# An attention kernel with head mixing and a dense block: a batch's second block scored a step sooner in its middle unit, heads 8 to 11 first, keys a step sooner

## Chip, cores and metric

One core of a Trainium2 chip. The metric is the device time of one execution in microseconds (us); lower is better. Engines are TensorE (PE, matmuls), VectorE (DVE), ScalarE (ACT), GpSimd (POOL) and SyncE (SP, which here only issues transfers).

## What is computed

For 4 batches, 12 heads, 448 positions and 64 dimensions per head, attention scores are mixed over the heads before the softmax and the weights once more after it; the result goes through a dense block of 768 to 2048 to 768 with an ELU between.

```python
scores = scale * np.matmul(q, k.transpose(0, 1, 3, 2))
scores = np.einsum('bhij,hg->bgij', scores, w_pre)
attn = exp(scores - max); attn = attn / (sum(attn) + 1e-09)
attn = np.einsum('bhij,hg->bgij', attn, w_post)
x = np.matmul(attn, v)              # (batch, head, position, 64)
h = x.reshape(1792, 768) @ w_in     # positions by heads and dimensions
out = elu(h) @ w_out
```

## The kernel before

The dense block (class `Moe`) runs after the attention and isn't touched by the change; the rest of this section is on `attention`.

**Blocks and steps.** The 448 query positions of a batch are cut into four blocks of 100, 120, 120 and 108 positions (`BLK`, in tiles of 10 rows). A block is worked off in steps of two tiles; the last step of a batch's fourth block has one tile. A batch is thus 5 + 6 + 6 + 6 = 23 steps (`ROUND`), the four batches 92 steps. Step numbers in this document are those of the round, 0 to 22, where nothing else is said. Batches, blocks and heads are counted from 0; "block 2" of a batch is its third.

**What a block goes through.** First its raw scores: for each of the six pairs of heads `qk` (line 220) multiplies the block's queries by the batch's keys. Both are split into a high and a low part, so three matmuls make one product. Two pairs are a unit: unit 0 has heads 0 to 3, unit 1 heads 4 to 7, unit 2 heads 8 to 11. `keep_qk` (line 230) copies the four results of a unit from PSUM into `st` tiles, two on DVE, then two on ACT. In the next step `send` (lines 242 and 245) moves them by transfers from SP into one of the two tiles `raw`, where the head becomes part of the partition; blocks alternate between the two. Head 11 goes in two halves (line 245), so unit 2 takes five transfers and the others four. Then, step by step, `scores` (line 256) mixes the heads of two tiles out of `raw`, the maximum is taken on DVE (`nm`, line 261), the exponential on ACT (`p`, line 263), `norm` makes the scaled weights `wz` on POOL (line 276), and `post` (line 287) applies the second mixing. `keep_post` (line 294) copies it to `at`. Last, `av` (line 308, results `xo`) multiplies by the values `v`, again in three units per block, and `keep_av` writes the block out.

**The order of the work.** One loop over the step number `j` issues everything. In iteration `j` PE gets the scores of step `j + 2`, then the `av` units of `avs[j]`, then the `qk` units of `qks[j]`, then the post-mix of step `j`; the transfers of the units of iteration `j - 1` are issued by SP behind the scores. So the first scores of a block are issued two iterations ahead of its first step, and need all three units of the block to have landed in `raw`. Two tables set the iterations: `RAW_AT` (line 377) has, for each block of a batch, the iterations of its three `qk` units relative to the batch's first step, `OUT_AT` (line 378) those of its three `av` units. Results of scores, `qk` and `av` take six PSUM banks in turn (`bank`): a step's scores two, an `av` unit one, a `qk` unit four.

**Keys and queries.** For each batch after the first, `load_k` (line 179) loads the keys of a pair of heads on POOL's queue, into four buffers, five iterations ahead of the unit that needs it; `split_k` makes `kh` on DVE (line 185) and `kl` on POOL (line 186) two and one iterations ahead. Queries go likewise through `load_q` (line 191) and `split_q` (line 198). The `v` tiles of the next batch are loaded on POOL's queue in iterations 23 to 28 (0 to 5 of the next round), and from iteration 8 on a decoder of the dense block's weights loads 512 KB (`w`) every eighth iteration or so.

The line in which a block's units are given their iterations:

```python
for u in range(2 if n == 1 else 0, 3):
    qks.setdefault(at[u], []).append((n, u))
```

Of the kernel before, what the change touches and what calls it, by code (L numbers as in the profile page):

```python
# [27 lines left out]
NP = H // 2  # L28
# [14 lines left out]
def f32(ap):  # L43
    return ap.bitcast(F32)
# [67 lines left out]
@with_exitstack  # L112
def body(ctx, tc, qd, kd, vd, wpre, wpost, w1d, w2d, outT):
    xd = [[tc.dram_tile([128, NC, nt * R], F32, name=f"xd{b}_{i}") for i, (_, nt) in enumerate(BLK)]
          for b in range(B)]
    s1 = [tc.dram_tile([128, PW], F32, name=f"s1_{i}") for i in range(w1d.shape[0])]
    s2 = [tc.dram_tile([128, PW], F32, name=f"s2_{i}") for i in range(w2d.shape[0])]
    todo = [(d[i], s[i]) for d, s in ((w1d, s1), (w2d, s2)) for i in range(d.shape[0])]
    dec = Weights(tc.nc, ctx.enter_context(tc.tile_pool(name="dec", bufs=2, side="right")), todo, tc.nc.gpsimd)
    with tc.manual_schedule():  # L120
        moe = Moe(ctx, tc, xd, s1, s2, dec, outT)
        attention(tc, qd, kd, vd, wpre, wpost, xd, dec, moe)
        moe.run()
# [3 lines left out]
def attention(ctx, tc, qd, kd, vd, wpre, wpost, xd, dec, moe):  # L127
    nc = tc.nc
# [48 lines left out]
    def load_k(b, hp, eng):  # L177
        k2[b, hp] = ld.tile([128, S], F32, tag="k2", name="k2", bufs=4)
        eng.dma_start(out=k2[b, hp], in_=kd[b, hp])

    def split_k(b, hp, high, low):
        src = k2.pop((b, hp))
        kh = kp.tile([128, S], F32R, tag="kh", name="kh")
        kl = kp.tile([128, S], F32R, tag="kl", name="kl")
        high(kh, src)
        low.tensor_sub(kl, src, f32(kh))
        ks[b, hp] = kh, kl

    def load_q(n, eng):
        q2[n] = ld.tile([128, NP, 120], F32, tag="q2", name="q2")  # L190
        eng.dma_start(out=q2[n], in_=qd[blocks[n]])

    def split_q(n, high, low):
        src = q2.pop(n)
        qh = qp.tile([128, NP, 120], F32R, tag="qh", name="qh")
        ql = qp.tile([128, NP, 120], F32R, tag="ql", name="ql")
        high(qh, src)
        low.tensor_sub(ql, src, f32(qh))
        qs[n] = qh, ql
# [168 lines left out]
    work, qks, avs = {}, {}, {}  # L368
    spare = mixes = six

    def plan(j, f):
        work.setdefault(max(j, -LOOK), []).append(f)
# [1 line left out]


    ROUND = sum(length)  // B
    RAW_AT = [(-10, -8, -6), (-4, -2, -1), (1, 3, 5), (7, 9, 11)]
    OUT_AT = [(6, 8, 10), (12, 14, 16), (18, 20, 22), (23, 25, 27)]
    for n in range(1, NBL):
        b, i = blocks[n]  # L380
        at = [b * ROUND + j for j in (RAW_AT[i] if n > 2 else (None, (0, 0, 0), (2, 4, 6))[n])]
        for u in range(2 if n == 1 else 0, 3):
            qks.setdefault(at[u], []).append((n, u))
        if n > 1:
            plan(max(at[0] - 5, 1 - LOOK), lambda n=n: load_q(n, nc.gpsimd))
        if n > 1:
            plan(at[0] - 2, lambda n=n: split_q(n, nc.vector.tensor_copy, nc.gpsimd))
        if i == (0 if b else 2):
            for hp in range(NP):
                if b:  # L390
                    plan(at[hp // 2] - 5, lambda b=b, hp=hp: load_k(b, hp, nc.gpsimd))
                plan(at[hp // 2] - 2 + hp % 2, lambda b=b, hp=hp: split_k(
                    b, hp, nc.vector.tensor_copy, nc.gpsimd))
    for n in range(NBL):
        b, i = blocks[n]
        for u, j in enumerate(OUT_AT[i]):
            j += b * ROUND
# [725 lines left out]
```

## Time and profile before

| what | value |
|---|---|
| median of 3 runs | 813.8 us (808.64 to 817.66) |
| the profiled execution | 816.36 us |
| its span, first to last instruction | 814.6 us |
| mean granted TensorE clock | 0.983 |
| PE busy | 779.7 us, 96% |
| DVE, ACT, POOL busy | 582.2, 510.1, 407.9 us (71, 63, 50%) |

Attention takes about the first 360 us of the span, the dense block the rest. A matmul of the code on these four-byte operands stands in the trace as two records, so the four score matmuls of a step are counted x8, a post-mix x56, an `av` unit x32. In a timeline the columns are start, duration (of the merged group), engine, line, operation, result and operands, shapes and count; in brackets the engine's idle time ahead of it and what ended it. "issue" means that the profile shows nothing that the engine waited for. `SPq` and `POOLq` are the queues of engines that issue transfers.

### The profile page before, as it was taken

How to read it: one execution, taken by the hardware profiler on the slowest of the kernel's cores; microseconds unless marked ns; L12 is line 12 of the kernel's file. 1: busy time of each engine (PE TensorE's matmuls, PEld its weight loads, DVE VectorE, ACT ScalarE, POOL GpSimd, SP SyncE). 2: the span in 40 equal slices, each digit the busy share in tenths (PEclk: the TensorE clock that was granted, in tenths of full speed). 3: DMA queues.
4: the chain of work that ended last, by engine and by line, in shares of the span. 5: the costliest groups of instructions: out<-in, count | busy, mean ns of one | idle time of the engine just before them, and what ended most of it. 6: DMA issues, size and time to landing. Idle time of an engine off the chain costs nothing.

```text
span 814.6 us, 25153 instructions
## 1 busy us (share of the span) xinstructions
PE 779.7 (96%) x10014; PEld 633.0 (78%) x10014; DVE 582.2 (71%) x1082; ACT 510.1 (63%) x1092; POOL 407.9 (50%) x529
## 2 busy tenths in 40 slices
PE   7788899899999999999999999999999999999998
PEld 3356577566666676678999999999999889899997
DVE  5676577597768777666988888776457777688962
ACT  3567678577777778786778783323157566665440
POOL 6565445374456543345777773266148777600000
PEclk9799899899999999999999999999999999999999
DMA  6568568665777676756988769987536867553331
GB/s 197 182 205 254 165 197 241 209 210 189 222 248 232 191 217 224 213 170 232 311 307 277 249 232 356 313 293 275 184 124 202 260 200 231 185 161 119 115 122 58
DMA packets 92845, 174.60 MB, mean 214 GB/s; under 512 B 21888, under 2 KB 59556, under 8 KB 92728
## 3 DMA queue, kind: packets, MB, share of 16 engines
q1 hardware_dynamic: 75288, 113.46, 43.4%
q0 software_dynamic: 16896, 58.61, 22.7%
q8 instruction: 79, 1.29, 0.7%
q10 hardware_dynamic: 544, 0.92, 0.3%
q14 instruction: 38, 0.31, 0.1%
HBM read 94.04 MB, written 39.35 MB: 164 GB/s over the span
## 4 chain that ended last, share of the span: by engine, by line
PE 82%; DMA 9%; DVE 3%; issue 2%; POOL 2%; ACT 2%; SPq 1%; POOLq 0%; ACTq 0%; DVEq 0%
PE h L595 14%; PE y L690 14%; PE y L1044 13%; PE h L982 10%; PE mixed L287 8%; PE s L256 8%; PE xo L308 8%; PE qk L220 6%; DMA raw<-st 3%; DMA sum<-mix 1%; ACT p L263 1%; DMA raw<-room 1%; DMA mix<-s 1%; DMA xl<-xd 1%; DMA wa<-in 1%
## 5 line engine op out<-in xcount | busy, mean ns | idle before, releaser
L263 ACT ACTIVATE p<-s,nm 128x448 f32<-128x448 f32 x180 | 113.0, 634 | 58.7 <-DVE nm L261 58.3
L261 DVE TENSOR_REDUCE nm<-s 128x1 f32<-128x448 f32 x180 | 103.8, 617 | 59.4 <-PE s L256 59.0
L276 POOL TENSOR_SCALAR wz<-wb,rz 128x60 f32<-128x60 f32 x180 | 80.4, 459 | 106.8 <-DVE rz L272 63.5
L294 ACT COPY at<-mixed 128x480 f32<-128x480 f32 (+1 forms) x184 | 93.4, 567 | 32.1 <-PE mixed L287 30.2
L256 PE MATMUL s<-raw,wa 64*64 64x448 f32 x720 | 95.8, 571 | 18.1 <-DMA raw<-st 9.1
L287 PEld LDWEIGHTS mixed<-wz,p 64*64 64x64 f32 x5040 | 86.3, 137 | 32.7 <-issue 24.7
L287 PE MATMUL mixed<-wz,p 64*64 64x60 f32 x5040 | 99.8, 225 | 5.1 <-issue 3.4
L308 PEld LDWEIGHTS xo<-at,v 128*64 128x64 f32 x1536 | 76.1, 135 | 33.0 <-ACT st L230 21.8
L1044 PE MATMUL y<-part,hi 128*128 128x448 f32 x336 | 96.4, 367 | 0.0
L308 PE MATMUL xo<-at,v 128*64 128x120 f32 (+2 forms) x1536 | 87.1, 263 | 0.5 <-issue 0.5
L511 ACT CAST hi<-lo 128x1024 fp32r<-128x1024 f32 (+1 forms) x49 | 48.1, 982 | 40.5 <-PE y L1044 34.5
L982 PE MATMUL h<-op,hi 128*128 128x448 f32 x264 | 72.2, 367 | 0.0
L595 PE MATMUL h<-xh,hi 128*128 128x448 f32 x192 | 70.7, 368 | 0.0
L595 PE MATMUL h<-xl,hi 128*128 128x448 f32 x192 | 70.1, 365 | 0.0
L595 PE MATMUL h<-xh,lo 128*128 128x448 f32 x192 | 70.1, 365 | 0.0
L690 PE MATMUL y<-gl,hi 128*128 128x448 f32 x192 | 69.8, 363 | 0.0
L690 PE MATMUL y<-gh,hi 128*128 128x448 f32 x192 | 69.8, 363 | 0.0
L690 PE MATMUL y<-gh,lo 128*128 128x448 f32 x192 | 69.7, 363 | 0.0
L982 PE MATMUL h<-op,lo 128*128 128x448 f32 x240 | 67.5, 368 | 1.4 <-POOL lo L839 1.4
L1044 PEld LDWEIGHTS y<-part,hi 128*128 128x128 f32 x336 | 63.0, 188 | 6.3
L512 DVE TENSOR_TENSOR lo<-lo,hi 128x1024 fp32r<-128x1024 f32 x30 | 37.5, 1250 | 40.6 <-ACT hi L511 38.4
L1044 PE MATMUL y<-part,lo 128*128 128x448 f32 x168 | 61.8, 368 | 0.0
(122 smaller groups left out, 1659.0 us busy)
## 6 DMA issues: line engine op xcount, KB each, us to landing
raw<-st SPq DMA_DIRECT2D x129, 210.0 KB
w<-in POOLq DMA_DIRECT2D x48, 512.0 KB, 5.8
lo<-s SPq DMA_DIRECT2D x58, 256.0 KB
s<-c POOLq DMA_DIRECT2D x48, 256.0 KB, 5.6
v<-in POOLq DMA_DIRECT2D x24, 256.0 KB, 6.3
lo<-half SPq DMA_DIRECT2D x16, 384.0 KB
lo<-sum SPq DMA_DIRECT2D x12, 512.0 KB
raw<-st SPq DMA_DIRECT2D x33, 175.0 KB
```

The costliest lines, as they stand in the source:

```text
L220: nc.tensor.matmul(got[hh][:m, :S], q[part, hp, :m], k[part], start=i == 0, stop=i == 2)
L256: nc.tensor.matmul(ps[a][w * 64:(w + 1) * 64, :S], wa[half], raws[n % 2][half, ts[0] + w, :], start=True, stop=True)
L261: nc.vector.tensor_reduce(nm, ps[i][:, :S], op=ALU.max, axis=AX.X, negate=True)
L263: nc.scalar.activation(p, ps[i][:, :S], AF.Exp, bias=nm, scale=1.0, accum_out=z[:, i:i + 1])
L276: nc.gpsimd.tensor_scalar_mul(wz, wb, rz[:, i:i + 1])
L287: nc.tensor.matmul(mixed[w][half, i, c, :], p[part, j * 64:(j + 1) * 64], wz[part], start=True, stop=True)
L294: nc.scalar.copy(ats[n][:, :, ts[0]:ts[0] + len(ts), w, :], mixed[w][:, :len(ts)].rearrange("p t c n -> p c t n"))
L308: nc.tensor.matmul(ps[hh * 64:(hh + 1) * 64, w * m:(w + 1) * m].rearrange("p (t r) -> p t r", r=HR), vs[blocks[n][0], hp][:, c, hh * 64:(h ...
L595: self.nc.tensor.matmul(h, w[:, ks], x[:, k, :], start=n == 0, stop=n == 3 * NC - 1)
L690: nc.tensor.matmul(y[u], w[:, ks], g[f][:, u, :], start=f == 0 and n == 0, stop=f == NF - 1 and n == 2)
L982: nc.tensor.matmul(y, p[:, ks], x[:, z], start=q < 2 and k == 0 and n == 0, stop=k == KH - 1 and n == 2, skip_group_check=True)
L1044: nc.tensor.matmul(y, w[:, ks], g[:, x], start=begun is None and k == 0 and n == 0, stop=k == FH - 1 and n == 2, skip_group_check=True)
```

## The change

Four parts:

- `RAW_AT` of a batch's block 1: its second unit is issued in iteration -3 instead of -2 (20 instead of 21 of the round).
- `OUT_AT` of block 2: its third `av` unit in 21 instead of 22.
- `UNITS = (2, 0, 1)`: from block 2 of the first batch on, each block's units are issued with heads 8 to 11 first, then 0 to 3, then 4 to 7, in the same iterations.
- Keys are loaded and split in that order, and for batches 1 to 3 one iteration sooner against the unit that needs them (`- bool(b)`).

```diff
-    RAW_AT = [(-10, -8, -6), (-4, -2, -1), (1, 3, 5), (7, 9, 11)]
-    OUT_AT = [(6, 8, 10), (12, 14, 16), (18, 20, 22), (23, 25, 27)]
+    RAW_AT = [(-10, -8, -6), (-4, -3, -1), (1, 3, 5), (7, 9, 11)]
+    OUT_AT = [(6, 8, 10), (12, 14, 16), (18, 20, 21), (23, 25, 27)]
+    UNITS = (2, 0, 1)
     for n in range(1, NBL):
         b, i = blocks[n]
-        at = [b * ROUND + j for j in (RAW_AT[i] if n > 2 else (None, (0, 0, 0), (2, 4, 6))[n])]
-        for u in range(2 if n == 1 else 0, 3):
-            qks.setdefault(at[u], []).append((n, u))
+        at = [b * ROUND + j for j in (RAW_AT[i] if n > 2 else (2, 4, 6))] if n > 1 else (None, None, 0)
+        for j, u in zip(at, (0, 1, 2) if n == 1 else UNITS):
+            if j is not None:
+                qks.setdefault(j, []).append((n, u))
...
         if i == (0 if b else 2):
-            for hp in range(NP):
+            for hp in (2 * u + w for u in UNITS for w in range(2)):
+                t = at[UNITS.index(hp // 2)] - bool(b)
                 if b:
-                    plan(at[hp // 2] - 5, lambda b=b, hp=hp: load_k(b, hp, nc.gpsimd))
-                plan(at[hp // 2] - 2 + hp % 2, lambda b=b, hp=hp: split_k(
+                    plan(t - 5, lambda b=b, hp=hp: load_k(b, hp, nc.gpsimd))
+                plan(t - 2 + hp % 2, lambda b=b, hp=hp: split_k(
                     b, hp, nc.vector.tensor_copy, nc.gpsimd))
```

How this moves instructions, at three places. On SP before, the transfers of a batch's block 3 (`raw_197`, batch 0), the write-out `xd` between them, and the first of the next batch's block 0 (`raw_196`):

```order
L242 DMA raw_197<-st 10x12x448 x8
L325 DMA xd_0_57<-x 128x600
L242 DMA raw_197<-st 10x12x448
L245 DMA raw_197<-st 5x12x448 x2
L242 DMA raw_197<-st 10x12x448 x2
```

And the same now:

```order
L242 DMA raw_197<-st 10x12x448
L245 DMA raw_197<-st 5x12x448 x2
L242 DMA raw_197<-st 10x12x448 x6
L325 DMA xd_0_57<-x 128x600
L242 DMA raw_197<-st 10x12x448 x4
```

The two half transfers of head 11 have moved from the last unit to the first; the last unit is four transfers. There are 13 for the block in both.

On PE before, step 22 of batch 0, ahead of its post-mix: the scores of two tiles, the third `av` unit of block 2 and the third `qk` unit of block 1 of the next batch. This was the step with both kinds of unit:

```order
L256 MATMUL s<-raw_196,wa 64x448 x4
L308 MATMUL xo<-at,v 64x120 x16
L220 MATMUL qk<-kh,qh 120x448 x2
L220 MATMUL qk<-kl,qh 120x448 x2
L220 MATMUL qk<-kh,ql 120x448 x2
L220 MATMUL qk<-kh,qh 120x448 x2
L220 MATMUL qk<-kl,qh 120x448 x2
L220 MATMUL qk<-kh,ql 120x448 x2
```

Now that step is 20, whose scores are of one tile (x2), with the second `av` unit of block 2 and the second `qk` unit of block 1:

```order
L256 MATMUL s<-raw_197,wa 64x448 x2
L308 MATMUL xo<-at,v 64x120 x16
L220 MATMUL qk<-kh,qh 120x448 x2
L220 MATMUL qk<-kl,qh 120x448 x2
L220 MATMUL qk<-kh,ql 120x448 x2
L220 MATMUL qk<-kh,qh 120x448 x2
L220 MATMUL qk<-kl,qh 120x448 x2
L220 MATMUL qk<-kh,ql 120x448 x2
```

The `av` unit that stood in step 22 is alone in step 21 now, and step 22 has the third `qk` unit alone.

On POOL before, steps 11 and 12 of batch 0, where the keys of batch 1 (`k_1073` and `k_1075` are the first pair loaded, `k_1404` and `k_1406` the third) are split and loaded, with the queries' `ql` and the step's `wz`:

```order
L198 TENSOR_TENSOR ql<-q_1071,qh 128x720
L186 TENSOR_TENSOR kl<-k_1073,kh 128x448
L276 TENSOR_SCALAR wz<-wb,rz 128x60 x2
L63 DMA w<-in 128x1024
L186 TENSOR_TENSOR kl<-k_1075,kh 128x448
L179 DMA k_1404<-in 128x448
L179 DMA k_1406<-in 128x448
```

Now, steps 10 and 11, with `k_993` and `k_995` the first pair and `k_1324` and `k_1326` the third:

```order
L63 DMA w<-in 128x1024
L186 TENSOR_TENSOR kl<-k_993,kh 128x448
L276 TENSOR_SCALAR wz<-wb,rz 128x60 x2
L198 TENSOR_TENSOR ql<-q_1076,qh 128x720
L186 TENSOR_TENSOR kl<-k_995,kh 128x448
L179 DMA k_1324<-in 128x448
L179 DMA k_1326<-in 128x448
```

The first `kl` stands a step ahead of `ql`, the second right behind it, and the third pair is loaded in the same step as `ql` instead of one later.

## Rows read from the trace of the kernel before

**Rows 1.** The list of PE's waits: who waited for whom, us, times, longest.
```profile
PE s L256 <- DMA raw<-st: 9.1, 5, 3.6
...
PE s L256 <- issue: 3.1, 1, 3.1
PE qk L220 <- POOL kl L186: 2.0, 4, 0.8
```

**Rows 2.** PE's timeline around the block awaited in batch 1.
```profile
145.13 1.04 PE L287 MATMUL mixed<-wz,p 64*64 64x60 f32 x56
...
148.43 1.04 PE L287 MATMUL mixed<-wz,p 64*64 64x60 f32 x56
153.03 1.77 PE L256 MATMUL s<-raw,wa 64*64 64x448 f32 x8 [3.57 <-DMA raw<-st]
...
161.49 1.04 PE L287 MATMUL mixed<-wz,p 64*64 64x60 f32 x56
```

**Rows 3.** PE's timeline: the other waits at a block's first scores.
```profile
88.59 1.77 PE L256 MATMUL s<-raw,wa 64*64 64x448 f32 x8 [3.08 <-issue]
...
238.50 0.98 PE L256 MATMUL s<-raw,wa 64*64 64x448 f32 x8 [1.42 <-DMA raw<-st]
...
299.35 0.98 PE L256 MATMUL s<-raw,wa 64*64 64x448 f32 x8 [0.41 <-DMA raw<-st]
...
320.36 0.98 PE L256 MATMUL s<-raw,wa 64*64 64x448 f32 x8 [1.35 <-DMA raw<-st]
```

**Rows 4.** The chain that ended last, ahead of 88.59: start, us, what.
```profile
76.00 10.40 DMA raw<-st
86.40 2.19 issue
```

**Rows 5.** Windows: stretch, us, busy time by engine, PE clock, DMA share, GB/s.
```profile
132.00:139.00 7.00, 7.00 (x194) 4.92 (x195) 5.10 (x13) 5.90 (x17) 2.75 (x6) 1.00 0.96 263
139.00:146.00 7.00, 7.00 (x225) 5.05 (x219) 5.92 (x16) 6.53 (x18) 3.91 (x6) 1.00 0.77 267
...
153.00:160.00 7.00, 6.97 (x86) 3.96 (x88) 3.25 (x7) 3.22 (x8) 0.91 (x3) 0.55 0.46 155
```

**Rows 6.** SP's timeline, single issues: first and last of three units.
```profile
100.67 0.78 SPq L242 DMA_DIRECT2D raw<-st  x1
...
104.09 0.78 SPq L242 DMA_DIRECT2D raw<-st  x1
108.93 0.76 SPq L242 DMA_DIRECT2D raw<-st  x1
...
111.49 0.76 SPq L242 DMA_DIRECT2D raw<-st  x1
...
139.12 0.78 SPq L242 DMA_DIRECT2D raw<-st  x1
...
143.78 0.78 SPq L242 DMA_DIRECT2D raw<-st  x1
```

**Rows 7.** PE's timeline in two double steps, step 6 and step 22 of batch 0.
```profile
52.71 0.46 PE L220 MATMUL qk<-kh,qh 64*120 64x448 f32 x1 [1.78 <-ACT p L263]
...
115.88 1.91 PE L308 MATMUL xo<-at,v 128*64 128x120 f32 x32
117.72 0.46 PE L220 MATMUL qk<-kh,qh 64*120 64x448 f32 x2
```

**Rows 8.** PE's timeline at the first unit of batches 2 and 3.
```profile
171.67 0.45 PE L220 MATMUL qk<-kl,qh 64*100 64x448 f32 x2 [0.44 <-POOL kl L186]
...
255.07 0.45 PE L220 MATMUL qk<-kl,qh 64*100 64x448 f32 x2 [0.76 <-POOL kl L186]
```

**Rows 9.** DMA issues: what, queue, count, size of one, median us to landing.
```profile
raw<-st SPq DMA_DIRECT2D x129, 210.0 KB
...
k<-in POOLq DMA_DIRECT2D x18, 224.0 KB, 6.7
```

**Rows 10.** POOL's timeline: the first keys of batch 2.
```profile
148.49 1.07 POOL L179 DMA_DIRECT2D k<-in  x2
```

## The prediction

> **What bounds the kernel now.** I began with the list of what TensorE (PE) waited for [rows 1], because PE is busy for 779.7 us of the span of 814.6 us (96%): what isn't PE work must show up there. The list is short. The largest row is the score matmuls of line 256 waiting for a transfer into `raw`, 9.1 us in 5 waits; beside it one wait of 3.1 us put down to "issue", and four waits of 2.0 us in all for `kl` from GpSimd (POOL). All of these lie in the attention part. The change touches nothing behind it except when the last transfer into `raw` is issued.
>
> Next I looked for the places of these waits in PE's timeline [rows 2, 3] and laid the planner's step numbers over it. The waits on `raw` stand before the first score matmuls of a block: at 88.59 us (block 3 of batch 0, issued in step 15 of the round), at 153.03, 238.50 and 320.36 us (block 2 of batches 1, 2 and 3, step 9), and a small one at 299.35 us (block 1 of batch 3, step 3). Four of the five of the list's first row are among these, 6.75 us; the other 2.35 us are in the start of batch 0, which isn't changed. The wait at 88.59 reads "issue" in the timeline, but the chain that ended last shows a transfer into `raw` of 10.40 us and 2.19 us of issue just ahead of it [rows 4], so I count it with them. A wait of 3.57 us costs more than 3.57 us: from the post-mix at 148.43 to that at 161.49 two steps take 13.06 us, where one ordinary step takes 3.30 us (145.13 to 148.43), so the excess is 13.06 - 6.60 = 6.5 us, 2.9 us more than the idle time. The windows say why: between 153 and 160 us the granted clock is 0.55, near the lower of its two levels (1.2 GHz), after 1.00 before the pause [rows 5]. The waits of 1.42 and 1.35 us weren't followed by such a stretch.
>
> Why are the transfers late? The queue of SyncE (SP) shows the last unit of a block being issued [rows 6]. Undisturbed, a unit with heads 8 to 11 takes five transfers (head 11 goes in two halves), 3.42 us from the first to the last issue (100.67 to 104.09); any other unit takes four and 2.56 us (108.93 to 111.49). The last unit of the block that was awaited at 153.03 was issued from 139.12 to 143.78, 4.66 us, and still needed some 9 us to land (143.78 to 153.03). From 132 to 139 us the DMA engines were 0.96 busy at 263 GB/s [rows 5]. So these waits are made of two things: when the last transfer is issued, and how full the engines are while it is under way.
>
> **The change, part by part.** The sum is made against the profiled execution's own 816.36 us (span 814.6 plus 1.8 around it). That is 2.6 us above the median of the three runs shown, 813.8.
>
> *Heads 8 to 11 first.* The five-transfer unit now opens a block and a four-transfer unit closes it. Bytes, matmuls and evictions are the same. The last issue comes 3.42 - 2.56 = 0.86 us sooner [rows 6]. If the landing is set only by how fast the engines drain the bytes queued ahead, the gain is 0; if it is set by the extra place in a queue as slow as at 139 to 144 us, one issue is worth 4.66 / 4 = 1.2 us. I take 0.86, the undisturbed difference, at each of the four large waits: 3.4 us, between 0 and 4.7. The wait of 0.41 us at 299.35 goes as well: 0.4. The same holds at the end, where the last block's last unit is one issue shorter, but PE doesn't wait for it: 0.
>
> *Second unit of a batch's second block a step sooner, and the third attention-times-values unit of its third block with it.* No work disappears. The step with both kinds of unit moves from step 22 to step 20 of the round. In the trace the double step runs through without a pause (xo at 115.88, qk at 117.72), while an earlier double step, the one near 50 us, waits 1.78 us for an exponential [rows 7]: a double step takes seven of the six PSUM banks in turn (two for scores, one for xo, four for qk), so its last one is the bank of its own first scores. Step 20 has one score tile instead of two, so the new double step takes six, and no bank comes round within it. I put it at 0; the bounds are a gain of nothing (there is no idle to win) and a loss of 3 x 1.78 = 5.3 us if all three new double steps paused like the early one. SP gets the first and second units of block 1 in neighbouring steps, and the third by itself; before, the second and third were neighbours. These are 840 KB (four of 210 KB, [rows 9]) moved ahead by one step of about 3.3 us. They leave the stretch where the loads of `v` begin, but the engines weren't full there, so I count nothing for the waits at step 9.
>
> *Keys split a step sooner.* PE waited for `kl` at 171.67 (0.44 us) and at 255.07 (0.76 us), both at the first unit of a new batch [rows 8]. With a whole step of about 3.3 us in hand both go: 1.2 us. What is next behind them is `ql`, made on POOL in the same step as before; it stood ahead of `kl` there and PE didn't wait for it, so the gain holds. The other two of the four waits are in batch 0, whose keys aren't moved. Could the cover be missing on the other side? The cast of `kh` now stands a step earlier on VectorE (DVE), but its load is a step earlier too, so the three steps between them (10 us) remain against a median of 6.7 us to landing [rows 9].
>
> *Keys loaded a step sooner.* This is the part that can cost something. In batch 1 the first pair was issued at 148.49 [rows 10], when the block awaited at 153.03 had been issued for nearly 5 us. Now it goes out some 3.3 us earlier, into the stretch where those transfers are still on their way. Two loads of 224 KB [rows 9] at 263 GB/s are 1.7 us of all the engines. The bound is therefore 1.7 us at each of the waits at 153.03 and 238.50, the other bound 0 (the pair was already beside them before). From 139 to 146 us the engines were 0.77 busy [rows 5], so there was room for most of it: 0.23 x 7 = 1.6 us. I take 0.5 each, 1.0 together. In batch 3 no keys follow, and in batch 0 a pair goes out beside the awaited transfers in either order: 0.
>
> The Trainium skill has a rule that speaks against this part: its page "DMA: Bandwidth & Descriptors", section "Issuing engines are not separate DMA queues", says that transfers started by SP and by POOL run on the same 16 engines and interleave. By that rule POOL's key loads take their share from SP's transfers into `raw`; the sum would then hold the full 1.7 us twice, and come to 2.4 us more than mine. The trace agrees that the engines are shared, in that they are 0.96 busy just where SP's issues stretch, and disagrees in size for the next 7 us, at 0.77.
>
> **The sum.** -3.4 - 0.4 - 1.2 + 1.0 = -4.0, so 816.4 - 4.0 = 812.4 for the profiled execution. A run at the median is 2.6 us shorter than this one, most likely by shorter waits of this very kind, and so has less to lose: 813.8 - 4.0 = 809.8 would be too much. I take 811, between the two.
>
> **The rivals.** *Nothing moves*, 814: landing is set by the bytes ahead, which don't change, and the key loads eat the 1.2 us. For it speaks that the last transfer was 9 us under way, far longer than its issue; against it that SP's own issues stretched from 3.42 to 4.66 us, so places in the queue count. Chance 0.27.
>
> *The large waits vanish with their slow clock*, 800 to 804: 6.5 us at 153.03, about 6 us at 88.59 (3.08 idle plus the same 2.9), 1.42 + 0.41 + 1.35 = 3.2 and 1.2 for the keys are 16.9 us; from 816.4 that is 799.5, and 804 where a median run has only part of these waits. For it speaks that waits of 1.4 us leave the clock alone, so that halving a wait can win the clock too; against it that 0.86 us is only a quarter of 3.57. Chance 0.15.
>
> *The key loads collide with the awaited block*, 818: the waits at 153.03 and 238.50 each grow by 1.7 us, and the second, now 3.1 us, is followed by a slow stretch as at 153 us, 2.9 us more. That is 6.3 us, less the 0.9 x 2 and 0.4 + 1.2 won elsewhere: +2.9 on the profiled run, 819, and 817 on the median; 818 between. It decides as soon as the engines stay full beyond 139 us, so that the pair's bytes have no gap to go into. For it speaks the 0.96 of the window before. Chance 0.13, and a third of it beyond 822.
>
> *The change doesn't do what it says*: the order of the instructions shows it on all engines, except that the double step isn't removed but moved. That alone would be 814 again and is in the first rival.
>
> **How the numbers follow.** My forecast, 808 to 813, has 0.45. One per cent, 8.1 us, is about what a measurement of this kernel can tell from no change: faster means below 805.7, slower above 821.9. Faster gets most of the second rival and a tail of the forecast: 0.15. Slower gets 0.05, from the third rival. The rest, 0.80, is the same. The range runs from 803 (the forecast's waits half gone, the clock won back once) to 818 (the collision); below and above I leave about a tenth each.
>
> **What would show it.** Right: on SP the two half transfers of line 245 are the first and not the last of a block, a block's last unit takes four issues; PE's waits on `raw` at the first scores of a block are shorter by about 1 us each, not gone; no wait for `kl` is left at the first unit of batches 2 and 3; PE runs through steps 20 to 22 without a pause. Wrong: a wait at step 9 of batch 1 or 2 that has grown, with POOL's key loads just ahead of it and the DMA share near 1; a wait on an exponential or a bank in step 20; a pause on DVE at the cast of `kh` for a late key; or waits on `raw` of unchanged length although their last issue is earlier. That last would say that the bytes ahead, not the order, set the landing.

## The result and the profile after

| | before | changed |
|---|---|---|
| median of 22 runs | 813.16 us (808.64 to 824.51) | 818.6 us (814.03 to 823.93) |
| ratio, 95% interval | | 1.006 [1.0037, 1.0082] |
| profiled execution, its span | 816.36 us, 814.6 us | 814.27 us, 812.5 us |
| mean granted TensorE clock | 0.983 | 0.985 |

The changed kernel is 0.6% slower, by about 5 us; 811 was predicted, and 818.6 lies 0.6 us above the range of 803 to 818. It is within the 1% that was given 0.80, but the interval lies on the other side of 1 from the forecast. A ratio here and below leaves out executions more than 1.5% above the fastest of their kernel, so it can differ from the quotient of the medians, and the traces of e5 and e16, which are of such executions, are not used.

Before any line is read, note the third row. The execution profiled before lies 3.2 us above its median, the one after 4.3 us below its own, so these two traces taken alone say that the change saves 2.1 us. One trace scatters here as much as the effect is large. The lines below show what happened; how much it is worth needs the medians and several traces, which follow with the experiments.

The list of PE's waits after, as [rows 1]: who waited for whom, us in total, times, longest.

```profile
PE s L256 <- DMA raw<-st: 9.6, 3, 6.5
...
PE xo L308 <- ACT st L230: 3.3, 2, 1.9
...
PE xo L308 <- ACT at L294: 1.2, 3, 0.4
...
PE qk L220 <- POOL kl L186: 0.4, 1, 0.4
```

Four rows, four readings. The waits for `kl` fell from 2.0 us in four to 0.4 in one: the two at the first units of batches 2 and 3, 1.2 us, are gone, as forecast of the splits (the one left is in batch 0, whose keys don't move). The waits of the scores on `raw` are fewer, but the longest grew from 3.6 to 6.5 us. And there are two rows that before has no like of: `xo` waiting for ACT's copy to `at`, three times exactly 0.40 us, and `xo` waiting for a copy to `st`. The last, 1.9 and 1.4 us at 135.80 and 308.17, is not explained here: neither comes back at its size in the two other traces of the changed kernel (e4 has none, e18 0.67 us at the second place).

The longest one is in batch 2, where [rows 3] had 1.42 us at 238.50. PE's timeline there (a step's post-mix, the awaited scores, the next post-mix):

```profile
225.71 1.36 PE L287 MATMUL mixed<-wz,p 64*64 64x60 f32 x56
233.55 1.77 PE L256 MATMUL s<-raw,wa 64*64 64x448 f32 x8 [6.48 <-DMA raw<-st]
...
237.77 1.76 PE L287 MATMUL mixed<-wz,p 64*64 64x60 f32 x56
```

From post-mix to post-mix this is 12.06 us, where a step takes 3.3. What surrounds it is in the windows (stretch, us, busy time of PE, PEld, DVE, ACT, POOL, granted clock, DMA share, GB/s):

```profile
219.00:226.00 7.00, 7.00 (x178) 4.86 (x174) 5.29 (x13) 5.53 (x15) 5.70 (x11) 1.00 0.87 285
226.00:234.00 8.00, 1.52 (x59) 1.23 (x62) 1.12 (x4) 2.13 (x6) 1.90 (x4) 0.73 0.79 236
234.00:242.00 8.00, 8.00 (x116) 4.98 (x108) 3.80 (x8) 4.00 (x11) 0.83 (x2) 0.63 0.35 111
```

The granted clock fell in the stretch with the pause (0.73) and was 0.63 in the one after it, as in [rows 5]: the scores and the post-mix of that step ran for 1.77 and 1.76 us instead of 0.98 and 1.04. So this wait cost 12.06 - 3.3 = 8.8 us, 2.3 more than its idle time.

Who was in the way? SP's queue has the awaited unit, four issues of which these are the first and the last, and no half transfer among them, as forecast ([rows 6] had five from 139.12 to 143.78):

```profile
216.18 0.78 SPq L242 DMA_DIRECT2D raw<-st  x1
...
219.04 0.76 SPq L242 DMA_DIRECT2D raw<-st  x1
```

POOL's timeline has the first two pairs of the next batch's keys:

```profile
222.29 1.13 POOL L179 DMA_DIRECT2D k<-in  x2
...
228.69 1.12 POOL L179 DMA_DIRECT2D k<-in  x2
```

The first pair goes out 3.25 us behind the last transfer that PE needs, and that transfer's scores begin 14.5 us after it was issued (219.04 to 233.55). Before, in the same place, the last issue was at 229.53, the keys came at 235.46, 5.9 us behind, and the scores began 9.0 us after the issue (238.50, [rows 3]):

```profile
229.53 0.78 SPq L242 DMA_DIRECT2D raw<-st  x1
...
235.46 1.07 POOL L179 DMA_DIRECT2D k<-in  x2
```

The DMA view splits the bytes by queue: q1 is SP's and q0 is POOL's (over the whole execution they move 113 and 59 MB, as much as SP and POOL issue). In the changed kernel, 219 to 223 us and then 223 to 229 us (packets, MB, share of the engines' time):

```profile
q1 hardware_dynamic: 468, 0.83, 57.4%
q0 software_dynamic: 92, 0.30, 22.0%
...
q0 software_dynamic: 289, 1.08, 57.1%
q1 hardware_dynamic: 354, 0.59, 29.9%
```

The engines moved as much per us in both, 287 and 278 GB/s. But SP's queue fell from 0.21 to 0.10 MB per us as soon as the keys were on the way, and POOL's took the rest. It moved 1.08 MB in those 6 us, more than twice the pair of keys (0.46 MB): the next block's queries (360 KB, issued at 224.61) and earlier loads were in the same queue.

The other new row stands at the seam of two batches. PE's timeline, steps 20 to 22 and the first of the next round:

```profile
101.52 1.90 PE L308 MATMUL xo<-at,v 128*64 128x120 f32 x32
103.36 0.47 PE L220 MATMUL qk<-kh,qh 64*120 64x448 f32 x2
...
108.56 1.04 PE L287 MATMUL mixed<-wz,p 64*64 64x60 f32 x56
...
111.70 0.68 PE L287 MATMUL mixed<-wz,p 64*64 64x60 f32 x28
112.21 1.30 PE L256 MATMUL s<-raw,wa 64*64 64x448 f32 x8
113.91 1.76 PE L308 MATMUL xo<-at,v 128*64 128x110 f32 x32 [0.40 <-ACT at L294]
```

The new double step 20 (101.52, 103.36) runs without a pause, as forecast. Iteration 22 is now only 3.14 us long for PE (108.56 to 111.70), since the `av` unit that stood in it is gone; ACT still has two exponentials, two copies to `st` and a copy to `at` to do there. The next step's `av` unit reads that `at`, and comes 0.40 us too early; the scores ahead of it are drawn out too, 1.30 us instead of 0.94. The same 0.40 stands at 197.57 and 286.70, and there is a wait of 0.75 us at the end of the attention, where the moved unit now stands in step 90 instead of 91 (counted through):

```profile
365.05 1.04 PE L287 MATMUL mixed<-wz,p 64*64 64x60 f32 x28 [0.75 <-ACT at L294]
```

### The profile page after: what moved, and what is told of

It is laid out like the page before. It is cut to its first block, busy times and chain, and to the rows that moved or that the text cites. A ratio compares the mean times of both kernels' runs of the same rounds, so it can differ in the third digit from the quotient of the medians.

```text
span 812.5 us, 25149 instructions
## 1 busy us (share of the span) xinstructions
PE 778.3 (96%) x10014; PEld 633.7 (78%) x10014; DVE 577.9 (71%) x1082; ACT 509.2 (63%) x1092; POOL 407.2 (50%) x529
## 4 chain that ended last, share of the span: by engine, by line
PE 81%; DMA 9%; ACT 4%; DVE 2%; issue 2%; POOL 1%; SPq 0%; POOLq 0%; DVEq 0%; ACTq 0%
PE h L598 14%; PE y L693 14%; PE y L1047 13%; PE h L985 13%; PE xo L308 7%; PE mixed L287 7%; PE s L256 6%; DMA raw<-st 6%; PE qk L220 5%; ACT p L263 2%; DMA raw<-room 1%; ACT at L294 1%; DVE rz L271 1%; DMA wa<-in 1%; DVE nm L261 1%
## 5 line engine op out<-in xcount | busy, mean ns | idle before, releaser
L294 ACT COPY at<-mixed 128x480 f32<-128x480 f32 (+1 forms) x184 | 93.4, 567 | 31.9 <-PE mixed L287 30.5
L287 PEld LDWEIGHTS mixed<-wz,p 64*64 64x64 f32 x5040 | 87.2, 138 | 31.4 <-issue 19.7
L514 ACT CAST hi<-lo 128x1024 fp32r<-128x1024 f32 (+1 forms) x49 | 48.0, 979 | 40.4 <-PE y L1047 34.6
```

The costliest lines, as they stand in the source:

```text
L287: nc.tensor.matmul(mixed[w][half, i, c, :], p[part, j * 64:(j + 1) * 64], wz[part], start=True, stop=True)
L294: nc.scalar.copy(ats[n][:, :, ts[0]:ts[0] + len(ts), w, :], mixed[w][:, :len(ts)].rearrange("p t c n -> p c t n"))
L514: self.nc.scalar.copy(hi_, f32(lo_))
```

## Experiments

Three explanations were open: the key loads, a step sooner, delay the transfers into `raw` (the collision, the third rival); the moved units cost PE time at the seam of the batches; or neither, the change is worth nothing and the rest is scatter. Diffs are against the kernel before where `-` lines are its lines, in the notation of the change; `UNITS = (0, 1, 2)` keeps the old order of units. Ratios are to the kernel before, measured beside it, with 95% intervals. Times of stretches are from the start of one step's post-mix to that of another, steps counted through all batches (a batch has 23, so 23, 46 and 69 are first steps).

### The parts one by one: e1_heads, e2_second, e3_keys, e4_all

Heads 8 to 11 first alone:

```diff
+    UNITS = (2, 0, 1)
-                t = at[UNITS.index(hp // 2)] - bool(b)
+                t = at[UNITS.index(hp // 2)]
```

(the last two lines against the changed kernel, whose two tables are as before here).

> Only the order of the heads (8 to 11 first); the iterations of the units and the keys' loads and splits as before, in the new order. If the order is the cause (the five-transfer unit now opens a block, so that the st tiles it filled come free later for the unit two further on): ratio to before 1.004 or more, and ACT's copies into st wait for transfers into raw for over 2 us in all (0.8 before). If the early key loads are the cause: 0.996 to 1.001, since the last unit of a block is one issue (0.86 us) shorter and nothing else changes. If the moved unit is the cause: the same.

Measured: 813.5 us, 0.9979 [0.9944, 1.0014]. The two tables alone:

```diff
-    RAW_AT = [(-10, -8, -6), (-4, -2, -1), (1, 3, 5), (7, 9, 11)]
-    OUT_AT = [(6, 8, 10), (12, 14, 16), (18, 20, 22), (23, 25, 27)]
+    RAW_AT = [(-10, -8, -6), (-4, -3, -1), (1, 3, 5), (7, 9, 11)]
+    OUT_AT = [(6, 8, 10), (12, 14, 16), (18, 20, 21), (23, 25, 27)]
```

> Only the second unit of a batch's block 1 and the third attention-times-values unit of block 2 a step sooner. If the moved unit is the cause: ratio 1.004 or more, with PE waits of about 0.4 us for the copy to at behind each double step (3 of them, 1.2 us) and SP's transfers of two neighbouring units late at steps 21 to 0. If the order of heads or the early key loads are the cause: 0.998 to 1.002, and the waits at step 9 stay near those of before (5.0 us in batches 1 and 2).

Measured: 817.33 us, 1.0037 [1.0005, 1.0069]. Keys loaded and split a step sooner alone:

```diff
-                    plan(at[hp // 2] - 5, lambda b=b, hp=hp: load_k(b, hp, nc.gpsimd))
-                plan(at[hp // 2] - 2 + hp % 2, lambda b=b, hp=hp: split_k(
+                t = at[hp // 2] - bool(b)
+                    plan(t - 5, lambda b=b, hp=hp: load_k(b, hp, nc.gpsimd))
+                plan(t - 2 + hp % 2, lambda b=b, hp=hp: split_k(
```

> Only the keys loaded and split a step sooner. If they collide with the transfers of the awaited block: ratio 1.004 or more, and the waits on raw at step 9 of batches 1 and 2 come to over 7 us together (5.0 before). If the order or the moved unit are the cause: 0.997 to 1.001, the two waits for kl at the first units of batches 2 and 3 (1.2 us) gone and the waits at step 9 as before.

Measured: 818.59 us, 1.0045 [1.0006, 1.0084]. Not as the collision asked: at step 9 of batches 1 and 2 its trace waits 1.75 us and nothing for `raw`; the long wait, 7.20 us, is in batch 0. The changed kernel once more beside them:

> The changed kernel itself once more, as the yardstick on this chip: ratio near 1.006, and a second profile of it, to see which of the waits of the first (6.48 us at step 9 of batch 2, 2.3 us at step 6 of batch 1, 2.19 us at step 9 of batch 0) come back. Waits that belong to the change come back in the same place; waits that are chance don't.

Measured: 818.6 us, 1.0061 [1.0023, 1.0099]. The parts multiply to the whole: 0.9979 x 1.0037 x 1.0045 = 1.0061. With intervals of 0.3 to 0.4% to each side so close an agreement is luck; but the second 1.006 puts scatter alone out, the heads have the forecast sign (their interval includes 1), and two parts seem to cost something: the tables and the keys.

### The two dear parts taken apart: e5_loads, e6_splits, e7_second_qk, e8_heads_splits

Only the loads sooner, for the first two of the three units' pairs, splits as before:

```diff
-                    plan(at[hp // 2] - 5, lambda b=b, hp=hp: load_k(b, hp, nc.gpsimd))
+                    plan(at[hp // 2] - 5 - (hp < 4), lambda b=b, hp=hp: load_k(b, hp, nc.gpsimd))
```

> Of the keys' part only the loads, and of these only the first two pairs of each batch, a step sooner; the splits, the order of heads and the units as before. If the loads collide with the awaited block: 1.003 to 1.008, with waits on raw at step 9 of batches 0 to 2 of over 7 us together (5.0 before), and the waits for kl still there. If the keys' cost lies in the splits (POOL or DVE kept busy at the wrong time) or was chance: 0.998 to 1.002.

Measured: 821.16 us, 1.0079 [1.004, 1.0119]. Only the splits sooner:

```diff
-                plan(at[hp // 2] - 2 + hp % 2, lambda b=b, hp=hp: split_k(
+                plan(at[hp // 2] - 2 - bool(b) + hp % 2, lambda b=b, hp=hp: split_k(
```

> Of the keys' part only the splits a step sooner, the loads as before, so that two steps instead of three lie between them. If the loads are the cause: 0.995 to 0.999, as the waits for kl go (1.2 us, up to 1.8 us over the steps 12 to 14) and no load moves. If the splits are the cause: 1.003 or more. If two steps aren't enough for a load, DVE waits for the keys at steps 10 to 15 and the step times there grow.

Measured: 814.42 us, 1.0044 [1.0006, 1.0082]; a miss. The median is only 0.2% above that of before beside it (812.95), and with the heads (e8, below) the same edit cost nothing, so whether it costs anything is open. Why it gains nothing is read from the traces: with the loads left in place only two steps lie between a load and its split. Steps 56 to 65, at the first units of batch 3, take 32.0 us with it, 31.4 before, and 30.6 where loads and splits both move (after, e3, e4). Only the second `qk` unit moved, `av` as before:

```diff
+    RAW_AT = [(-10, -8, -6), (-4, -3, -1), (1, 3, 5), (7, 9, 11)]
     OUT_AT = [(6, 8, 10), (12, 14, 16), (18, 20, 22), (23, 25, 27)]
```

> The second unit of a batch's block 1 a step sooner, but the third attention-times-values unit of block 2 left in step 22, which so keeps both kinds of unit, as step 20 now has. If the cost of the moved unit comes from the short step 22 (ACT copies at late, 0.40 us at each of three steps 0, some 0.7 us from step 19 to 24) and from the unit moved from step 91 to 90 at the end (0.85 us): both go, and the ratio is 0.998 to 1.001. If it comes from the transfers issued earlier: 1.002 to 1.005 stays.

Measured: 813.95 us, 0.9999 [0.9965, 1.0033]. So the cost of e2 goes with the `av` unit, not with the `qk` unit; the stretches below show the same without the scatter of whole executions. Heads and splits together (`UNITS` of e1, the split of e6):

```diff
+    UNITS = (2, 0, 1)
+                plan(t - 2 - bool(b) + hp % 2, lambda b=b, hp=hp: split_k(
```

> Heads 8 to 11 first and the keys' splits a step sooner, with the loads and the units where they were: what is left if the loads and the moved unit are the two costs. By that theory 0.993 to 0.998 and faster than both kernels; if the interplay of all transfers, not a part, sets the time: 0.998 to 1.004.

Measured: 812.99 us, 0.9983 [0.9945, 1.0021], that is e1 with nothing added; that it would beat the kernel before was expected and is not shown.

### Loads the other way: e9_loads_late, e10_heads_late

If sooner is worse, is later better? Loads four steps ahead, in the kernel before and with heads first:

```diff
-                    plan(at[hp // 2] - 5, lambda b=b, hp=hp: load_k(b, hp, nc.gpsimd))
+                    plan(at[hp // 2] - 4, lambda b=b, hp=hp: load_k(b, hp, nc.gpsimd))
```

> The opposite sign: the kernel before with the keys loaded a step later (four iterations ahead of their unit instead of five), splits, heads and units as before. If the early loads cost time by standing beside the transfers of the awaited block, later loads should save some: 0.993 to 0.999, the waits on raw at step 9 shorter and those for kl as before or longer. If the loads are at their best place in the kernel before: 1.000 to 1.005, as keys come late for their split.

> Heads 8 to 11 first together with the later loads: the candidate to beat both kernels if the loads are the cause, 0.991 to 0.997; 0.998 to 1.003 if only the total of transfers counts.

Measured: 814.66 us, 1.0031 [0.9998, 1.0064], and 818.51 us, 1.0058 [1.002, 1.0095]; the second, taken for the candidate to beat both kernels, is a miss. PE now waits for the late keys' `kl` at the first unit of each of the three batches; its timeline in e9:

```profile
83.06 0.44 PE L220 MATMUL qk<-kl,qh 64*100 64x448 f32 x2 [1.59 <-POOL kl L186]
...
167.98 0.45 PE L220 MATMUL qk<-kl,qh 64*100 64x448 f32 x2 [1.41 <-POOL kl L186]
...
251.94 0.45 PE L220 MATMUL qk<-kl,qh 64*100 64x448 f32 x2 [1.77 <-POOL kl L186]
```

Five steps ahead, the place before the change, looks like the best of the three: later and the keys are late, sooner and `raw` is. The later loads are shown to cost something only with heads first (e10 against e1 and e8); e9's interval includes 1.

### Two repeats: e11_loads_again, e12_before_again

The kernel of e5, and the kernel before against itself:

> The earlier loads alone once more, for a second measurement and another profile: 1.004 to 1.011 and waits on raw at step 9 of batches 0 to 2 of over 7 us together if the loads are the cost; below 1.003 if the first measurement was chance.

> The kernel before against itself: 0.997 to 1.003, which shows what a ratio of so many runs can tell, and a second profile of it: the waits that stand in both profiles belong to the kernel, the others to the execution.

Measured: 820.32 us, 1.0092 [1.0057, 1.0128], and 812.06 us, 1.0017 [0.9979, 1.0055]. The loads alone cost 0.8 and 0.9%, as much as the whole change or more. Their trace has what the collision asks for, PE's waits at the first scores of block 2 in batches 0, 1, 2, long ones, and a short one in batch 3, where no keys follow:

```profile
66.31 1.77 PE L256 MATMUL s<-raw,wa 64*64 64x448 f32 x8 [5.80 <-DMA raw<-st]
...
153.15 1.77 PE L256 MATMUL s<-raw,wa 64*64 64x448 f32 x8 [4.17 <-DMA raw<-st]
...
243.55 1.77 PE L256 MATMUL s<-raw,wa 64*64 64x448 f32 x8 [6.84 <-DMA raw<-st]
...
327.11 0.98 PE L256 MATMUL s<-raw,wa 64*64 64x448 f32 x8 [0.42 <-DMA raw<-st]
```

Only the last scores ran for 0.98 us; after the three long waits they took 1.77. (Batch 3 is not always free: e14 waits 2.57 us there.) The kernel before, run again, has none of these in batches 0 and 1 and 0.62 us in batch 2, so even the 3.57 us of [rows 2] were not in every execution; and a wait of 5.34 us at that place stands in e2, whose loads are not moved.

### Parts taken out of the change: e13_undo_loads, e14_undo_av, e15_undo_both

Against the changed kernel, the loads put back to where they were, then the `av` unit, then both:

```diff
-                    plan(t - 5, lambda b=b, hp=hp: load_k(b, hp, nc.gpsimd))
+                    plan(t - 4, lambda b=b, hp=hp: load_k(b, hp, nc.gpsimd))
-    OUT_AT = [(6, 8, 10), (12, 14, 16), (18, 20, 21), (23, 25, 27)]
+    OUT_AT = [(6, 8, 10), (12, 14, 16), (18, 20, 22), (23, 25, 27)]
```

> The changed kernel with the key loads put back where they were, and all else kept (heads order, moved units, splits a step sooner). If the early loads are a cost within the change too: 1.000 to 1.004, that is 2 to 5 us below the changed kernel, and no wait on raw of over 4 us at step 9 of batches 0 to 2. If the loads cost only when they stand alone: 1.005 to 1.008.

> The changed kernel with the third attention-times-values unit of block 2 put back into step 22 (and 91 at the end), all else kept. If that unit costs some 3 us as between the earlier pair: 1.001 to 1.005, with 18.3 instead of 18.95 us from step 19 to 24 and 7.65 instead of 8.45 us from step 89 to 91. If not: 1.005 to 1.008.

> The changed kernel with both put back: heads 8 to 11 first, the second unit of block 1 a step sooner and the splits a step sooner. If the two parts are all that the change costs: 0.995 to 1.000, no slower than the kernel before, and the candidate to beat both. If something else in the change costs: 1.002 or more.

Measured: 813.25 us, 1.0007 [0.9982, 1.0032]; 816.66 us, 1.0033 [1.0, 1.0066]; 812.25 us, 0.9946 [0.9908, 0.9985]. The loads put back take back most of it, and both together all of it; the `av` unit put back gives 0.28% against e4, which the intervals don't tell from nothing (its cost is read from the stretches). In e15's trace the wait at block 2 is 0.55 us in batch 0, and none in batches 1 and 2 (e17, the same kernel: 1.56, none, 1.87):

```profile
61.94 0.98 PE L256 MATMUL s<-raw,wa 64*64 64x448 f32 x8 [0.55 <-DMA raw<-st]
...
233.95 0.98 PE L256 MATMUL s<-raw,wa 64*64 64x448 f32 x8
```

and the first keys of batch 3 go out on POOL 8.6 us behind the awaited unit's last issue (223.76):

```profile
232.40 1.07 POOL L179 DMA_DIRECT2D k<-in  x2
```

At the seam of the batches e14 and e15 have no wait for `at`. In e14 the next step's `av` unit follows on post-mix and scores (not shown) without idle time:

```profile
118.03 0.62 PE L287 MATMUL mixed<-wz,p 64*64 64x60 f32 x26
...
118.48 0.22 PE L287 MATMUL mixed<-wz,p 64*64 64x60 f32 x2
...
119.41 1.77 PE L308 MATMUL xo<-at,v 128*64 128x110 f32 x32
```

### The last repeats: e16_heads_again, e17_undo_both_again, e18_all_again

> The order of heads alone once more, to pool with the first measurement (0.998): 0.995 to 1.000 if a last unit that is one issue shorter saves time, 0.999 to 1.003 if the landing is set by the bytes ahead and the order saves nothing.

> The kernel of e15 once more: 0.993 to 0.999 if it beats the kernel before; 0.999 to 1.002 if the first measurement was at the lucky end.

> The changed kernel on the same chip beside it: 1.004 to 1.009, so that the two put-back parts are worth 0.7 to 1.3% between the two kernels of this pair.

Measured: 810.67 us, 0.9978 [0.9941, 1.0015]; 812.2 us, 0.9984 [0.9947, 1.0021]; 816.95 us, 1.0037 [0.9999, 1.0075]. The heads come out as in e1. The version without the two dear parts is 4.75 us, 0.6%, below the changed kernel on the same chip, less than the 0.7 to 1.3% expected; against the kernel before, its two measurements (0.9946 and 0.9984, by the medians 0.998 and 0.9985) say not slower, and at best some tenths of a per cent faster. That it beats before is not settled.

### The stretches over all traces

| stretch, us | `-` before, e12 | e15, e17 | loads sooner: after, e18, e14, e11, e4, e3 | `av` moved: after, e18, e4, e13, e2 |
|---|---|---|---|---|
| steps 0 to 9 | 36.0, 35.4 | 35.0, 35.6 | 38.7, 40.4, 42.5, 41.6, 41.7, 43.3 | |
| steps 10 to 19 | 38.3, 35.7 | 36.0, 36.4 | 30.6, 30.6, 30.6, 31.3, 30.6, 30.6 | |
| steps 52 to 55 | 11.8, 10.7 | 10.1, 12.3 | 18.7, 18.2, 18.4, 18.1, 14.6, 10.7 | |
| steps 19-24, 42-47, 65-70, 89-91, sum | 62.6, 63.2 | 62.8, 62.6 | | 65.3, 65.4, 65.3, 65.4, 65.7 |

The lowest row is as clean as a trace gets. The thirteen traces with the `av` unit in its place take 62.6 to 63.8 us, and the pairs that differ in it alone (e4, e18 and after against e14, e13 against e15 and e17, e2 against e7) are 2.6 to 3.0 us apart. The wait for `at` stands at all three seams in the five with the unit moved, and of the thirteen others in three (e1, e8, e10), at the first seam alone.

The rows on the loads scatter more than four traces of comparison show. Over all ten with the loads in their place, steps 0 to 9 take 35.0 to 40.4 us (e13 39.5, e6 40.4), so that row overlaps; its middle is 36.5, against 41.7 in the six with the loads sooner. Steps 52 to 55 take 10.1 to 13.8, which only e3 of the six comes down to. And the second row goes the other way: in steps 10 to 19, with the loads in their place, PE mostly has pauses that are gone with the loads sooner (30.5 to 38.3 us, middle 35.7, against 30.6). In batch 0 the earlier loads so win back most of what they lose, 76.3 against 74.8 us over steps 0 to 19; what stays is the wait in batch 2.

SP's queue shows the sharing more evenly than the waits do. In the 4 us behind the last issue of batch 0's block 2 it moved 66 to 101 KB per us in the six traces, and 121 to 167 in all with the loads in their place or later. For batch 2 one can also set, trace by trace, the last issue of the awaited unit against the first key load and the scores:

| trace | keys go out behind the last issue | scores begin behind it |
|---|---|---|
| before, e12, e13, e17 | 5.9, 6.2, 6.6, 6.7 us | 9.0, 8.5, 10.1, 10.2 us |
| e15 | 8.6 | 10.2 (no wait) |
| after, e18, e14, e11 | 3.3, 3.5, 3.4, 2.6 | 14.5, 14.7, 14.4, 13.8 |
| e4 | 4.5 | 14.4 (PE itself late by an "issue" pause) |
| e3 | 3.7 | 9.7 |

e3 is the exception: there batch 2 went free, and its cost lies in batch 0 (a wait of 7.20 us). The traces not in the table, e1, e2, e6 and e7, have their keys 6.0 to 7.9 us behind and the scores 9.1 to 10.4; in e8 PE itself was late.

## Why the prediction was wrong

**The key loads** (taken at +1.0, bound 1.7 at each of two waits): this is the step that failed most, the price of the collision with the awaited block. Alone they cost 0.79 and 0.92%, 6 to 8 us; taken out of the change, they give back 0.54% (e4 to e13) or 0.3% (e18 to e13). Three things were wrong in the term. Its bound was the pair's own bytes by the bandwidth, 1.7 us; the wait in batch 2 grew by 5 us (1.42 before, 6.48 after, 6.84 in e11), so the bytes don't bound the delay. The trace shows SP's queue at half its rate, with the awaited transfers still under way, while POOL's moved the keys and the queries behind them. Batch 0 was put at 0, since "a pair goes out beside the awaited transfers in either order"; but it now goes out while they are under way (POOL at 54.50, SP's issues until 55.39) and not after, and waits of 2.19 to 7.20 us came there (with the loads in their place 0 to 4.70). That the batch loses only some 1.5 us over steps 0 to 19 all the same is luck: the prediction had no term for the pauses in steps 10 to 19. And the long waits (4.17 us and more in e11, 6.48 after) were followed by matmuls at the slow clock, which the sum left to a rival. The third rival had the mechanism, one of its two places (batch 2; in batch 1 the change's three traces wait 0.92 to 3.02 us, less than the 3.57 of before) and nearly the time, 818. The time is partly luck, since 2.7 us of what was measured are the `av` unit's. It got 0.13 because the DMA share of 0.77 after 139 us was read as room. A share below 1 didn't mean that an awaited transfer went unhindered: it was 0.79 during the longest wait.

The rule that the prediction cited against this part, the Trainium skill's page "DMA: Bandwidth & Descriptors", section "Issuing engines are not separate DMA queues", pointed the right way: transfers started by POOL do get in the way of SP's. The queue sums above agree, with SP's rate halved; and the loads alone cost more, 6 to 8 us, than the twice 1.7 us that the prediction worked out beside the rule.

What sets the split between the two queues is not shown. POOL's packets are about twice as large (0.30 MB in 92, against 0.83 MB in 468 of SP's from 219 to 223 us), which is a lead. The loads were moved, not shortened or cut into other sizes, so whether their packets, their order on the engines or their source in memory matters stays open.

**The moved `av` unit** (taken at 0, with 0 to 5.3 as its bounds): 2.7 us by the stretches. Of the whole kernel that is a third of a per cent, near the limit of the ratios: 0.37% with the `qk` unit (e2; 0.2% by the medians), 0.28% between e4 and e14. The question put to it was the wrong one. The prediction asked whether the new double step 20 would run out of PSUM banks, and it doesn't. It didn't ask what the step that loses the unit had used it for: the `av` unit in step 22 was PE work under which ACT caught up with the copies to `at` and `st`. "No work disappears" was true, but cover did.

**Heads first** (taken at -3.8): 0.9979 and 0.9978, about -1.7 us, though each interval includes 1: the gain is likely, not shown. The issues on SP are as forecast; but the prediction applied 0.86 us to four waits read from one execution, and before's second trace has none of the four over 0.80 us.

**The splits** (taken at -1.2): right inside the change. The waits for `kl` at batches 2 and 3 are gone, and steps 33 to 36 with 56 to 65 take 40.4 us in after, e3 and e4 (41.1 and 41.5 in e18 and e14) instead of 42.2. It holds only together with the loads; "its load is a step earlier too" was the condition, and where it is dropped (e6, e8) the gain is gone.

**The sum.** With measured terms: -1.7 for the heads, +2.7 for the `av` unit, +3.7 for loads and splits together (e3, 0.45%), is +4.7; from 813.16 that is 817.9, against 818.6. The two terms from ratios are uncertain by some 3 us each, so the agreement says no more than that nothing large is missing.

## What to carry to other kernels

Before loading something sooner, look at what is on the way at the new place and who waits for it: two prefetches moved by one step, onto transfers that PE waited for, cost more than their bytes at full bandwidth, for the other queue fell to half its rate; and a DMA share below 1 was no sign of room. When a unit of work is moved off a step, ask which other engine used its time as cover, not only whether it fits where it goes. Of a kernel whose runs scatter by two per cent (808.64 to 824.51 here), take waits from several traces before any is given a price.

## What was not expected of the hardware

Pauses of PE that the profile puts down to nothing ("issue") of 1 to 4 us come and go from one execution to the next. The kernel before, profiled again, was 4.6 us shorter (span 810.0 us) with this list of PE's waits:

```profile
PE mixed L287 <- issue: 7.8, 6, 1.8
...
PE xo L308 <- issue: 3.2, 1, 3.2
...
PE s L256 <- DMA raw<-st: 1.4, 2, 0.8
```

Against [rows 1] the waits for `raw` fell from 9.1 to 1.4 us and all of PE's "issue" pauses together grew from 7.0 to 11.0, in one and the same program.

The packet records say what they most likely are. One DMA queue, which the DMA view calls `instruction`, moves 16 KB in one packet every 5 us or so. Of the 60 "issue" pauses above 0.8 us between 30 and 370 us of the 18 traces, 58 end 1.2 to 1.7 us after such a packet has ended; a moment picked at random lies so in one case of eleven. So PE seems to have waited for its own instructions to be loaded. In steps 10 to 19 such pauses stand in eight of the ten traces with the key loads in their place and in none of the six with the loads sooner, so the data on the other queues may well be what makes the instructions late. No run was made to test it.
